# Block linear attention into an ELU feed-forward on one core: uncast loads for the first chunks, k decayed once, a plain causal mask, and a new order of all work

## The chip, the core and the metric

The kernel runs on one of the eight cores of a Trainium2 chip. A core has TensorE (PE in the profile), which multiplies matrices into PSUM; VectorE (DVE), ScalarE (ACT) and GpSimd (POOL) for elementwise work; SyncE (SP), which here only issues DMAs; and 16 DMA engines. Each engine executes its own instructions in order and waits on semaphores for the others. The metric is the device time of one execution in microseconds, lower is better.

## The reference, cut to what matters

q, k and v have 4 batches, 8 heads, 768 positions and 64 columns; `lam` is one decay per head. The output has 3072 rows (batch times position) of 512 columns.

```python
for b in range(nb):                                   # blocks of 64 positions
    intra = einsum('bhic,bhjc->bhij', qb, kb) * Dmask   # lam**(i-j) where i >= j, else 0
    intra = einsum('bhij,bhjd->bhid', intra, vb)
    inter = einsum('bhid,bhde->bhie', qb * lam_pow, kv_state)   # lam**(i+1)
    out[:, :, sl] = intra + inter
    kv_state = lam_block * kv_state + einsum('bhsd,bhse->bhde', kb * rev_pow, vb)
x = out.transpose(0, 2, 1, 3).reshape(B * S, H * D)     # 3072 x 512
h = x @ w_in                                            # 512 x 2048
g = where(h > 0, h, exp(minimum(h, 0)) - 1)
return g @ w_out                                        # 2048 x 512
```

## The kernel before

The work is cut into 24 chunks of 128 positions: chunk g is row `g // 4` of batch `g % 4`. Chunks 0 to 3 are the first row and have no incoming state. Chunks 0 to 3 are loaded and multiplied one by one, all later ones in pairs (4 and 5, 6 and 7, and so on).

For one chunk the steps are: q and k are transposed, chunks 0 to 7 on TensorE (`att_T_pe`, L274) with ScalarE copying k and VectorE multiplying q by its decay `qs`, later chunks by DMA (`att_T_dma`, L264). `att_S` (L294) computes the scores in two PSUM banks; `att_E` (L313) multiplies each by the mask, which holds the causal zeros and k's part of the decay. `att_P` (L327) multiplies by v and adds q times the state. The result is copied to `xt`. `att_kd` (L169) makes on GpSimd a second, decayed k, and `att_U` (L388) multiplies it with v for the next state; `att_M` (L368) multiplies the old state by its decay on GpSimd, and VectorE adds the two (L412).

The feed-forward takes `xt` in units. A unit `mm1(g0, j)` (L467) is eight or sixteen matmuls into one `psH` bank, for which there are two buffers; ScalarE then makes exp and relu (L484, L485), and VectorE joins them into `g` (L457). A unit `mm2(g, j)` (L490) is four matmuls of 512 columns over four tiles of g, added in one bank per chunk; four units finish a chunk, and the output is copied and stored.

w_in and w_out arrive in eight pieces each (`i0` to `i7`, `o0` to `o7`), two column tiles (row tiles for w_out) in a piece. A piece `i` serves a half of a single chunk's mm1 unit: unit j needs i(2j) and i(2j+1). A mm2 unit j needs o(2j) and o(2j+1). All these loads, and those of q, k, v, are issued by GpSimd with a cast from fp32 to fp16 on the way; the one exception is q of chunk 0, loaded uncast by SyncE and cast by VectorE.

The schedule is written by hand. `POOL_ORDER` (L47) orders GpSimd's loads (`k0`, `i0`, ...), decayed k (`d`) and state decay (`m`). `OPEN` (L53) orders the rest up to chunk 8: T, S, P, U, W, `1:g:j` and `2:g:j`; from there offsets (`AT`, L63) place each step relative to the mm1 units. VectorE's evacuations stand in a list `late` and are emitted one by one between the units. `w2` and `w6` in `OPEN` are two and six matmuls of zeros (L84), besides ten at the start. `BANKS` names the PSUM bank of each early tile.

Of the kernel before, what the change touches and what calls it, by code (L numbers as in the profile page):

```python
# [15 lines left out]
def kernel(  # L16
# [30 lines left out]
    POOL_ORDER = (  # L47
        "k0 k1 iota q1 k2 v1 i0 v0 q2 i1 v2 i2 o0 i3 d0 q3 o1 i4 k3 i5 o2 o3 v3 d1 m4 d2 d3 i7 "
        "o4 o5 i6 o7 k4 o6 q4 m5 k6 v4 q6 k10 q10 d5 d4 d6 m6 v6 k8 q8 v8 d7 m7 v10"
    )  # L50
    RAW = "q0"
    FIRST = "q0:0 c0 c1 c2"
    OPEN = (  # L53
# [7 lines left out]
    )  # L61
    LAGU = 7
    AT = {"L": -18, "W": -13, "T": -9, "S": -8, "B": -4}  # L63
    BANKS = (
        "S0=M0,M1 S1=C,D S2=D,M1 S3=D,B P0=M1 P1=B P2=B P3=D U0=M0 U1=D U2=A U3=M1 T0=M1,C "
        "T1=D,A T2=A,D T3=D T4=M0 T5=A T6=M1 T7=D M2=C M3=M0"
# [14 lines left out]
    def zero_matmuls(n):  # L81
# [4 lines left out]
    zero_matmuls(10)  # L86
# [4 lines left out]


# [3 lines left out]
    st = [  # L96
        [cpool.tile([128, NHP, 128], FP16, name=f"st{b}_{i}") for i in range(2)]
        for b in range(B)
    ]
    qg, kg, vg = {}, {}, {}  # L100

    def emit_load(w, g0):
        n = size_of[g0]
        c, b = divmod(g0, B)
        x = {"q": q, "k": k, "v": v}[w]
        src = x[b : b + n, :, c * L : (c + 1) * L].rearrange("b h p d -> p (b h) d")
        t = asb.tile([128, n, H, 64], FP16, tag=f"{w}n{n}", name=f"{w}n{g0}", bufs=4)
        {"q": qg, "k": kg, "v": vg}[w][g0] = t
        nc.gpsimd.dma_start(out=t[:].rearrange("p b h d -> p (b h) d"), in_=src)  # L109


    raw = {}
    for w in RAW.split():
        x = {"q": q, "k": k}[w[0]]
        g0 = int(w[1:])
        raw[w] = asb.tile([128, H, 64], FP32, name=f"raw_{w}", tag=f"raw_{w}")
        (nc.sync if w[0] == "q" else nc.scalar).dma_start(
            out=raw[w][:], in_=x[g0, :, 0:L].rearrange("h p d -> p h d")
        )
    nc.scalar.preload_act_table_set("natural_log_exp_and_others")  # L120

    def cast_raw(g, w, eng):
        n = f"{w}{g}"
        t = asb.tile([128, 1, H, 64], FP16, tag=f"{w}n1", name=f"{w}n{g}", bufs=4)
        (qg if w == "q" else kg)[g] = t
        if eng == 0:
            nc.vector.tensor_copy(t[:, 0], raw[n][:])
        else:
            nc.scalar.copy(t[:, 0], raw[n][:])

    def of(tiles, g):
        g0, i = group_of[g]
        return tiles[g0][:, i]
# [29 lines left out]
    def emit_iota():  # L163
        nc.gpsimd.iota(iota_c[:], pattern=[[0, 1]], base=0, channel_multiplier=1)
        nc.gpsimd.iota(iota_r[:], pattern=[[1, 128]], base=0, channel_multiplier=0)

    kds, qkT, Pt, psS, xg = {}, {}, {}, {}, {}

    def att_kd(g):  # L169
        if g // B == NCB - 1:  # L170
            return
        kd = asb.tile([128, H, 64], FP16, tag="kd", name=f"kd{g}", bufs=8)
        kds[g] = kd
        nc.gpsimd.tensor_tensor(  # L174
            out=kd[:], in0=of(kg, g),
            in1=ks[:].unsqueeze(2).broadcast_to([128, H, 64]), op=ALU.mult,
        )


    pool_list = POOL_ORDER.split()  # L180

    def emit_pool():
        w = pool_list.pop(0)
        if w == "iota":
            emit_iota()
        elif w[0] in "qkv":
            emit_load(w[0], int(w[1:]))
        else:
            {"i": emit_wi, "o": emit_wo, "d": att_kd, "m": lambda g: att_M(g)}[w[0]](int(w[1:]))

    def emit_pool_run():
        while pool_list and pool_list[0][0] != "m":
            emit_pool()

    assert "iota" in POOL_ORDER.split("d0")[0]
    while pool_list and pool_list[0][0] not in "dm":
        emit_pool()

    def zero_st1(b):
        nc.vector.memset(st[b][1][:], 0.0)  # L200


    loglam = cpool.tile([128, H], FP32, name="loglam")
    nc.scalar.activation(loglam[:], lam_b[:], AF.Ln)
    pos = cpool.tile([128, 3], FP32, name="pos")
# [4 lines left out]

    dn = cpool.tile([128, H], FP32, name="dn")
    mask = cpool.tile([128, H, 128], FP32, name="mask")
    qs = cpool.tile([128, NHP, 128], FP32, name="qs")
    ks = cpool.tile([128, H], FP32, name="ks")
    upp = cpool.tile([128, NHP], FP32, name="upp")
    nc.vector.tensor_copy(row[:], iota_r[:])
    nc.vector.tensor_copy(pos[:, 0:1], iota_c[:])
    nc.vector.tensor_scalar_mul(pos[:, 1:2], iota_c[:], -1.0)
    nc.scalar.activation(dn[:], loglam[:], AF.Exp, scale=pos[:, 1:2])
    nc.vector.tensor_scalar(  # L220
        out=ident16[:], in0=row[:], scalar1=pos[:, 0:1], scalar2=None, op0=ALU.is_equal
    )
    nc.vector.tensor_scalar(
        out=causT[:], in0=row[:], scalar1=pos[:, 0:1], scalar2=None, op0=ALU.is_ge
    )
    for hh in range(2):
        r = slice(hh * 64, (hh + 1) * 64)
        nc.vector.tensor_copy(loglam_p[r, :], loglam[r, hh::2])
    nc.vector.tensor_scalar_add(pos[:, 2:3], pos[:, 1:2], float(L))

    def emit_qs():
        for hp in range(NHP):
            nc.scalar.activation(
                qs[:, hp, :], row[:], AF.Exp, scale=loglam_p[:, hp : hp + 1]
            )

    def emit_mask():
        nc.vector.tensor_tensor(
            out=mask[:],
            in0=causT[:].unsqueeze(1).broadcast_to([128, H, 128]),  # L240
            in1=dn[:].unsqueeze(2).broadcast_to([128, H, 128]),
            op=ALU.mult,
        )

    def emit_ks():
        nc.scalar.activation(ks[:], loglam[:], AF.Exp, scale=pos[:, 2:3])
        nc.scalar.activation(upp[:], loglam_p[:], AF.Exp, scale=float(L))

# [13 lines left out]


    def att_T_dma(g):  # L264
        ts = []
        for w, tiles in (("q", qg), ("k", kg)):
            t = asb.tile([128, NHP, 128], FP16, tag=f"{w}T", name=f"{w}T{g}", bufs=6)
            nc.sync.dma_start_transpose(
                out=t[:], in_=of(tiles, g).rearrange("p h d -> p (h d)")
            )  # L270
            ts.append(t)
        qkT[g] = ts

    def att_T_pe(g):  # L274
        n = len(TAGS[f"T{g}"].split())
        pts = [
            bank(f"T{g}", i, [128, 2 // n, NHP, 128], FP16, f"psT{g}_{i}")
            for i in range(n)
        ]
        pts = [pts[0][:, 0], pts[n - 1][:, 2 // n - 1]]  # L280
        for src, pt in zip((of(qg, g), of(kg, g)), pts):
            for hp in range(NHP):
                nc.tensor.transpose(  # L283
                    pt[:, hp, :], in_=src[:, 2 * hp : 2 * hp + 2, :], identity=ident16[:]
                )
        qt, kt = [
            asb.tile([128, NHP, 128], FP16, tag=f"{w}T", name=f"{w}T{g}", bufs=6)
            for w in "qk"
        ]
        nc.vector.tensor_tensor(out=qt[:], in0=pts[0], in1=qs[:], op=ALU.mult)  # L290
        nc.scalar.copy(out=kt[:], in_=pts[1])  # L291
        qkT[g] = (qt, kt)

    def att_S(g):  # L294
        qt, kt = qkT[g]
# [11 lines left out]
    late, X_done, Y_done, E_done = [], set(), set(), set()  # L307

    def until(done, g):
        while g not in done:  # L310
            late.pop(0)()

    def att_E(g):  # L313
        pts = psS.pop(g)

        def half(hh):
            P = asb.tile([128, NHP, 128], FP16, tag="pp", name=f"pp{g}_{hh}", bufs=6)
            nc.vector.tensor_tensor(  # L318
                out=P[:], in0=pts[hh][:], in1=mask[:, hh::2, :], op=ALU.mult
            )  # L320
            Pt[(g, hh)] = P
            if hh == 1:
                E_done.add(g)

        return [lambda: half(0), lambda: half(1)]

    def att_P(g):  # L327
        cb, b = divmod(g, B)
        until(E_done, g)
        if cb > 0:  # L330
            until(Y_done, g - B)
# [331 lines left out]
```

## Time and profile before

| | us |
|---|---|
| device time, three runs | 215.18, 215.49, 215.70 (median 215.49) |
| span of the profiled execution, first to last instruction | 213.2 |
| PE busy | 202.7 (95%) |
| DVE, ACT, POOL busy | 130.1, 129.0, 96.2 |
| read from and written to HBM | 27.27 MB and 6.29 MB |

The profiled execution has no device time beside it other than these runs; its span lies 2.3 us below their median. In what follows, a row of a timeline gives the start, the length, the engine, the line, the operation, the tiles and the count of instructions that were merged; brackets at the end give idle time before it and what ended that. A row of TensorE ends some 0.17 us after its last issue, so the distance between the starts of two rows is what the first one costs.

### The profile page before, as it was taken

The page shows a single profiled execution, that of the slowest core. Times are in us where ns is not written, and L with a number is a line of the kernel's source. Part 1 is how long each engine was busy: PE and PEld are TensorE (multiplying, and loading weights), DVE is VectorE, ACT ScalarE, POOL GpSimd, SP SyncE. Part 2 cuts the span into 40 slices and gives each one's busy share as a digit, 9 for nine tenths or more (in the row PEclk, how much of TensorE's full clock was granted, in tenths as well). Part 3 has the DMA queues.
Part 4 walks back from the last instruction along what each step waited for, and adds up shares of the span by engine and source line. Part 5 has one row for each costly group of instructions (what it writes and reads, how often), then busy time and mean ns, then how long its engine had stood idle before and what let it go on. Part 6 is the DMA issues. An engine that isn't in the chain of part 4 may idle for free.

```text
span 213.2 us, 5156 instructions
## 1 busy us (share of the span) xinstructions
PE 202.7 (95%) x2066; PEld 138.1 (65%) x2066; DVE 130.1 (61%) x224; ACT 129.0 (61%) x245; POOL 96.2 (45%) x115
## 2 busy tenths in 40 slices
PE   7667999999999999999999999999999999999994
PEld 2355676767686776766766766766766666666652
DVE  3936453777846888677667667667667547533321
ACT  4545654884867756676476476476476576477640
POOL 7996991999972908667166259300000000000000
PEclk9999999999999999999999999999999999999999
DMA  8999999999996999999939919999124110110112
GB/s 90 141 175 193 192 148 173 147 165 147 153 165 145 111 197 107 144 122 116 129 106 125 167 59 103 144 180 161 52 65 83 52 49 0 54 51 16 36 49 98
DMA packets 101976, 24.59 MB, mean 115 GB/s; under 512 B 92608, under 2 KB 99008, under 8 KB 101952
## 3 DMA queue, kind: packets, MB, share of 16 engines
q0 software_dynamic: 79760, 13.50, 83.1%
q1 hardware_dynamic: 22192, 10.76, 24.6%
q8 instruction: 16, 0.26, 0.5%
q14 instruction: 8, 0.07, 0.1%
HBM read 27.27 MB, written 6.29 MB: 157 GB/s over the span
## 4 chain that ended last, share of the span: by engine, by line
PE 82%; POOL 8%; DMA 7%; issue 1%; ACT 1%; DVE 0%; POOLq 0%; ACTq 0%
PE psM L499 36%; PE psH L478 35%; DMA wi<-in_moe_w_in_dram 4%; DMA wo<-in_moe_w_out_dram 3%; PE psO L338 3%; PE psS L302 3%; PE psO L344 2%; POOL kd L174 1%; POOL wi L148 1%; POOL kn L109 1%; POOL vn L109 1%; PE psU L406 1%; PE psT L283 1%; POOL qn L109 1%; POOL wo L155 1%
## 5 line engine op out<-in xcount | busy, mean ns | idle before, releaser
L478 PE MATMUL psH<-xt,wi 128*128 128x256 f16 (+1 forms) x896 | 99.3, 258 | 2.0 <-DMA wi<-in_moe_w_in_dram 1.1
L457 DVE SCALAR_TENSOR_TENSOR g<-e,psH 128x512 f16<-128x512 f32 x96 | 65.8, 686 | 56.7 <-ACT psH L485 56.0
L484 ACT ACTIVATE e<-psH 128x512 f32<-128x512 f32 x96 | 57.3, 597 | 65.0 <-PE psH L478 62.8
L499 PE MATMUL psM<-wo,g 128*128 128x512 f16 (+1 forms) x384 | 95.6, 377 | 0.7 <-DMA wo<-in_moe_w_out_dram 0.7
L478 PEld LDWEIGHTS <-wi 128*128 128x128 f16 x896 | 76.9, 98 | 27.4 <-DMA wi<-in_moe_w_in_dram 1.8
L485 ACT ACTIVATE psH<-psH 128x512 f32<-128x512 f32 x96 | 57.0, 593 | 0.0
L499 PEld LDWEIGHTS <-g 128*128 128x128 f16 x384 | 35.9, 98 | 29.3 <-issue 1.3
L318 DVE TENSOR_TENSOR pp<-psS,mask 128x512 f16<-128x512 f32 x48 | 30.8, 684 | 4.4 <-PE psS L302 4.4
L174 POOL TENSOR_TENSOR kd<-kn,ks 128x512 f16<-128x512 f16 x20 | 20.7, 1040 | 21.3 <-DMA kn<-in_k_dram 20.4
L378 POOL TENSOR_TENSOR stt<-st,upp 64x256 f32<-64x256 f16 x32 | 19.5, 608 | 14.7 <-DVE st L418 8.9
L109 POOL DMA_DIRECT2D vn<-in_v_dram x14 | 15.5, 1108 | 1.7 <-DMA wi<-in_moe_w_in_dram 1.7
L109 POOL DMA_DIRECT2D kn<-in_k_dram x14 | 15.5, 1105 | 0.8 <-POOLq L647 0.8
L525 ACT COPY osb<-psM 128x512 f32<-128x512 f32 x23 | 13.5, 590 | 3.2 <-PE psM L499 3.2
L109 POOL DMA_DIRECT2D qn<-in_q_dram x13 | 14.8, 1138 | 0.0
L418 DVE TENSOR_TENSOR st<-stt,psU 64x256 f16<-64x256 f32 x32 | 13.3, 416 | 1.2 <-PE psU L406 0.5
L361 DVE TENSOR_TENSOR xt<-psO,qs 128x512 f16<-128x512 f32 x16 | 11.0, 688 | 3.5 <-PE psO L344 3.5
L338 PE MATMUL psO<-pp,vn 128*64 128x128 f16 x192 | 12.0, 222 | 1.2 <-DMA vn<-in_v_dram 1.0
L338 PEld LDWEIGHTS <-vn 128*64 128x64 f16 x192 | 9.7, 110 | 4.6 <-issue 2.9
L344 PE MATMUL psO<-qT,st 128*64 128x128 f16 x160 | 10.0, 219 | 0.0
L344 PEld LDWEIGHTS <-st 128*64 128x64 f16 x160 | 8.9, 110 | 0.0
L302 PE MATMUL psS<-qT,kT 64*128 64x128 f16 x192 | 7.9, 218 | 0.3 <-ACT kT L291 0.3
L359 ACT CAST xt<-psO 128x512 f16<-128x512 f32 x8 | 4.4, 588 | 6.4 <-PE psO L338 4.3
(44 smaller groups left out, 72.3 us busy)
## 6 DMA issues: line engine op xcount, KB each, us to landing
out_dram<-osb SPq DMA_DIRECT2D x23, 256.0 KB, 2.2
kn<-in_k_dram POOLq DMA_DIRECT2D x10, 256.0 KB, 7.8
qn<-in_q_dram POOLq DMA_DIRECT2D x10, 256.0 KB, 6.8
vn<-in_v_dram POOLq DMA_DIRECT2D x10, 256.0 KB, 7.6
wi<-in_moe_w_in_dram POOLq DMA_DIRECT2D x8, 256.0 KB, 6.9
wo<-in_moe_w_out_dram POOLq DMA_DIRECT2D x8, 256.0 KB, 7.7
kn<-in_k_dram POOLq DMA_DIRECT2D x4, 128.0 KB, 4.2
vn<-in_v_dram POOLq DMA_DIRECT2D x4, 128.0 KB, 5.5
```

The source lines that it names most:

```text
L109: nc.gpsimd.dma_start(out=t[:].rearrange("p b h d -> p (b h) d"), in_=src)
L174: nc.gpsimd.tensor_tensor(out=kd[:], in0=of(kg, g), in1=ks[:].unsqueeze(2).broadcast_to([128, H, 64]), op=ALU.mult,)
L302: nc.tensor.matmul(psS[g][hh][:, hp, :], lhsT=kt[r, hp, :], rhs=qt[r, hp, :], start=True, stop=True,)
L318: nc.vector.tensor_tensor(out=P[:], in0=pts[hh][:], in1=mask[:, hh::2, :], op=ALU.mult)
L338: nc.tensor.matmul(po[r, hp, :], lhsT=vt[:, 2 * hp + hh, :], rhs=Pt[(g, hh)][:, hp, :], start=True, stop=(cb == 0), skip_group_check=True,)
L344: nc.tensor.matmul(po[r, hp, :], lhsT=st[b][cb % 2][:, hp, r], rhs=qt[:, hp, :], start=False, stop=True, skip_group_check=True,)
L378: nc.gpsimd.tensor_tensor(out=tmp[r], in0=old[r, :, r], in1=upp[r].unsqueeze(2).broadcast_to([64, NHP, 64]), op=ALU.mult,)
L457: nc.vector.scalar_tensor_tensor(out=g[:].rearrange("p f c t -> p (f c t)"), in0=e[:], scalar=-1.0, in1=r[:], op0=ALU.add, op1=ALU.min,)
L478: nc.tensor.matmul(pH[:, f * n * 128 : (f + 1) * n * 128], lhsT=wi16[i][:, kk, w * 128 : (w + 1) * 128], rhs=xg[g0][:, kk, :], start=(kk = ...
L484: nc.scalar.activation(e[:], pH[:], AF.Exp)
L485: nc.scalar.activation(pH[:], pH[:], AF.Relu)
L499: nc.tensor.matmul(psM[g][:, cols], lhsT=gts[(g, j * FB + f)], rhs=wo16[i][:, w, cols], start=first and f == 0, stop=end and f == FB - 1, ...
```

## The change

Four things change. q of chunks 0 to 3 (SyncE's queue) and k of chunks 0 and 1 (ScalarE's queue) are loaded uncast and multiplied by their decay on VectorE or GpSimd (`scaled`). The decayed k is also what is transposed for the scores, so k's decay is made once, and its base is the chunk's end; the mask is then causal alone, the same for all heads. The state is added first (`att_Y`, VectorE) and multiplied by the decay after that (`att_M`, GpSimd). And one list, `ORDER`, gives the place of every step of every engine, with no offsets and no `late`; it has no zero matmuls but the ten at the start. `BANKS` names all banks.

The tokens of `ORDER`: `L:k2` a cast load, `i:3` and `o:4` weight pieces, `a:q1:v` uncast q or k times decay (`v` VectorE, `p` GpSimd, `a` ScalarE, here and below), `d:5:p` decayed k from a cast k, `t:k4` and `D:k8` a transpose on TensorE or by DMA, `e:k4:a` the transpose's copy out of PSUM, `s`, `p`, `u` the TensorE steps S, P and U, `E:4:1` one half of the mask, `x` the copy to `xt`, `y` and `m` the two steps of the state, `z` zeros into a state tile, `1:g:j` and `2:g:j` the units, `g:g:j` the joining into g. The other words are constants.

```diff
-    RAW = "q0"
+    ZEROS = 10
+    RAW = "q0S k0A q1S k1A q2S q3S"
+    ORDER = (
+        "z:2:1:a i:3 L:k2 iota L:v1 log row col caus ks logp ident a:k0:v t:k0 qn a:q0:p z:0:1:a t:q0 e:k0:a "
+        "a:q1:v L:v0 e:q0:a a:k1:p i:2 L:k3 s:0 E:0:1 i:1 t:q1 e:q1:a i:0 qs:2 L:v2 i:4 i:5 t:k1 e:k1:a E:0:0 "
+        "L:k4 qs:3 a:q2:v s:1 E:1:1 z:1:1:a qs:0 E:1:0 d:2:v L:q4 t:q2 u:1 a:q3:v L:v3 z:1:0:v i:6 e:q2:a p:1 "
+        "t:k2 u:0 upp x:1:a p:0 i:7 L:v4 t:q3 y:1 L:q6 o:4 d:5:p e:k2:a s:2 y:0 o:5 L:k6 o:0 o:2 E:2:0 E:2:1 "
+        "x:0:a o:3 d:3:v 1:0:1 1:1:1 g:0:1 o:1 t:k3 e:q3:v e:k3:a 1:0:0 g:1:1 p:2 d:7:p u:2 1:1:0 x:2:v o:6 "
+        "y:2 s:3 g:0:0 1:0:2 E:3:0 g:1:0 E:3:1 o:7 1:2:0 d:4:v t:k4 t:k5 e:k4:a g:0:2 L:k8 qs:1 L:q8 g:2:0 "
+        "z:3:1:v e:k5:a 1:2:1 t:q4 D:q8 t:q5 e:q4:v e:q5:v 1:1:2 u:3 p:3 x:3:a s:5 g:2:1 E:5:0 s:4 1:0:3 "
+        "g:1:2 L:q10 E:4:1 1:2:2 E:4:0 u:4 g:0:3 p:4 u:5 1:3:3 E:5:1 t:q7 g:2:2 x:4:v L:v6 t:q6 y:3 z:0:0:v "
+        "g:3:3 d:9:p e:q6:v 1:3:2 L:v8 g:3:2 p:5 y:5 x:5:a y:4 L:q12 L:k12 d:8:p 2:2:2 1:3:0 d:6:v L:k10 "
+        "1:1:3 2:0:2 t:k7 g:3:0 g:1:3 t:k6 2:1:2 1:2:3 1:3:1 L:v12 2:2:1 2:0:0 g:2:3 g:3:1 1:4:2 D:q9 2:0:1 "
...
+        "2:4:2 g:6:4 2:6:0 2:5:1 y:7 m:7 2:6:2 g:6:7 2:6:1 D:k11 m:9 2:4:3 1:8:0 s:10 s:11 E:10:0 E:10:1 "
+        "g:8:0 E:11:0 2:6:3 E:11:1 1:8:1 g:8:1 2:7:0 1:8:2 g:8:2 2:7:1 1:8:3 d:12:p D:q12 D:k12 g:8:3 1:8:4 "
...
+    )
...
+    for w in RAW.split():
+        g0 = int(w[1:-1])
+        raw[w[:-1]] = asb.tile([128, H, 64], FP32, name=f"raw_{w[:-1]}", tag=f"raw_{w[:-1]}")
+        {"S": nc.sync, "A": nc.scalar}[w[-1]].dma_start(
+            out=raw[w[:-1]][:], in_=xin[w[0]][g0, :, 0:L].rearrange("h p d -> p h d")
+        )
...
+    def scaled(w, g, eng):
+
+        t = asb.tile([128, H, 64], FP16, tag="kd" if w == "k" else "qd", name=f"{w}d{g}", bufs=8 if w == "k" else 4)
+        {"v": nc.vector, "p": nc.gpsimd}[eng].tensor_tensor(
+            out=t[:], in0=raw[f"{w}{g}"][:],
+            in1=(ks if w == "k" else qn)[:].unsqueeze(2).broadcast_to([128, H, 64]), op=ALU.mult,
+        )
...
+    def att_T_pe(w, g):
+        pt = bank(f"T{w}{g}", 0, [128, NHP, 128], FP16, f"psT{w}{g}")
+        src = of("q", g) if w == "q" else kds[g][:]
...
-                out=P[:], in0=pts[hh][:], in1=mask[:, hh::2, :], op=ALU.mult
...
+    def att_E(g, hh):
+        P = asb.tile([128, NHP, 128], FP16, tag="pp", name=f"pp{g}_{hh}", bufs=6)
+        nc.vector.tensor_tensor(
+            out=P[:], in0=psS[g][hh][:],
+            in1=causT[:].unsqueeze(1).broadcast_to([128, NHP, 128]), op=ALU.mult,
+        )
...
+            nc.gpsimd.tensor_tensor(
+                out=new[r, :, r], in0=stt.pop((g, hh))[r],
+                in1=upp[r].unsqueeze(2).broadcast_to([64, NHP, 64]), op=ALU.mult,
+            )
+
+    def att_Y(g, hh):
...
+        if cb == 0:
+            nc.vector.tensor_tensor(
+                out=stp[b][1][r, :, r], in0=src,
+                in1=upp[r].unsqueeze(2).broadcast_to([64, NHP, 64]), op=ALU.mult,
+            )
+        else:
+            tmp = asb.tile([128, NHP, 64], FP32, tag="stt", name=f"stt{g}_{hh}", bufs=8)
+            nc.vector.tensor_tensor(
+                out=tmp[r], in0=stp[b][cb % 2][r, :, r], in1=src, op=ALU.add
+            )
...
+    for t in ORDER.split():
+        run(t)
+    mm2_rest()
+    emit_stores()
```

More of the change, by code (lines that the diff above doesn't have):

```diff
@@ L161 @@
     iota_r = cpool.tile([128, 128], I32, name="iota_r")
[L163 to L200, printed above, removed]
     loglam = cpool.tile([128, H], FP32, name="loglam")
-    nc.scalar.activation(loglam[:], lam_b[:], AF.Ln)
-    pos = cpool.tile([128, 3], FP32, name="pos")
+    col = cpool.tile([128, 2], FP32, name="col")
     row = cpool.tile([128, 128], FP32, name="row")
@@ L219 @@
[L219 to L242, printed above, removed]
[L243 to L247 removed]
+    def emit_iota():
+        nc.gpsimd.iota(iota_c[:], pattern=[[0, 1]], base=-L, channel_multiplier=1)
+        nc.gpsimd.iota(iota_r[:], pattern=[[1, 128]], base=-L, channel_multiplier=0)
@@ L305, in att_S @@
                 )
[L307 to L318, printed above, removed]
-                out=P[:], in0=pts[hh][:], in1=mask[:, hh::2, :], op=ALU.mult
[L320 to L325, printed above, removed]
+    def att_E(g, hh):
[4 more added lines that the diff above has]
+        )
+        Pt[(g, hh)] = P
     def att_P(g):
         cb, b = divmod(g, B)
-        until(E_done, g)
-        if cb > 0:
-            until(Y_done, g - B)
-        vt = of(vg, g)
-        qt, _ = qkT[g]
+        vt = of("v", g)
+        qt = qkT[("q", g)]
         po = bank(f"P{g}", 0, [128, NHP, 128], FP32, f"psO{g}")
@@ L397, in att_U @@
+    def att_U(g):
+        if g < B:
+            pu = bank(f"U{g}", 0, [128, NHP, 64], FP32, f"psU{g}")
+        elif g % 2 == 0:
+            psUU[g] = bank(f"U{g}", 0, [128, 2, NHP, 64], FP32, f"psU{g}")
+            pu = psUU[g][:, 0]
+        else:
+            pu = psUU[g - 1][:, 1]
+        vt = of("v", g)
+        for hp in range(NHP):
+            for hh in range(2):
+                r = slice(hh * 64, (hh + 1) * 64)
                 nc.tensor.matmul(
-                    full[:, hp, :].rearrange("p (h e) -> p h e", h=2),
@@ L585 @@
-    for t in FIRST.split():
-        run(t)
-    emit_pool_run()
-    prog = OPEN.split()
-    done = set(prog) | {o for t in prog if t[0] == "B" for o in t.split(":")}
-    m1 = [(g, j) for g, n in GSIZE.items() for j in range(NJ * n)]
-    place = {u: i for i, u in enumerate(m1)}
-    need = {
-        (g, j): place[(GFIRST[g], ((j + 1) * FB - 1) // (FB // GSIZE[GFIRST[g]]))]
-        for g in range(NG) for j in range(NJ)
-    }
-    m2 = [(g, j) for g in range(NG) for j in range(NJ) if f"2:{g}:{j}" not in done]
@@ L612 @@
-    m1 = [x for x in m1 if "1:%d:%d" % x not in done]
-    first = place[m1[0]]
-    for p in sorted(extra):
-        if p < first:
-            prog += extra.pop(p)
-    for x, (g, j) in enumerate(m1):
-        u = first + x
-        prog.append(f"1:{g}:{j}")
-        prog += extra.pop(u, [])
-        n = 2
-        while m2 and need[m2[0]] <= u - 2 and n and len(m2) - (len(m1) - 1 - x) > LAGU:
-            prog.append("2:%d:%d" % m2.pop(0))
-            n -= 1
-    for g, j in m2:
-        prog.append(f"2:{g}:{j}")
```

354 lines of the change are left out of this document (130 added, 224 removed), and 41 rows, old and new, of tables (BANKS, OPEN, ORDER).

## The prediction

> **What bounds the kernel now.** I read the page first, then the chain of waits, then the timeline engine by engine, and last the time from issue to landing of each load. Page, 40 slices of 5.33 us:
>
> ```profile
> PE   7667999999999999999999999999999999999994
> PEclk9999999999999999999999999999999999999999
> DMA  8999999999996999999939919999124110110112
> ```
>
> TensorE is full from the fifth slice on, at full clock. Before that it is short of work, while the DMA engines are full for the first 64 us. The chain of waits says for what:
>
> ```profile
> 11.63 8.79 DMA wi<-in_moe_w_in_dram
> ...
> 27.49 6.73 DMA wo<-in_moe_w_out_dram
> 34.26 1.46 PE psM L499 x6
> ```
>
> The TensorE timeline: the first w_in product starts at 13.37 us, the last wait over 0.25 us on a load ends at 34.26, and from then on rows follow each other, with one gap of 0.22 us at 87.
>
> ```profile
> 13.37 0.61 PE L478 MATMUL psH<-xt,wi 128*128 128x128 f16 x8
> ...
> 34.26 1.46 PE L499 MATMUL psM<-wo,g 128*128 128x512 f16 x6 [0.35 <-DMA wo<-in_moe_w_out_dram]
> ...
> 43.23 0.39 PE L283 MATMUL psT<-ident,kn 128*128 128x128 f16 x4
> 43.45 1.03 PE L499 MATMUL psM<-wo,g 128*128 128x512 f16 x4
> ```
>
> So the span is the opening plus a remainder that runs at TensorE's pace. From chunk 8 on the new order is regular, with the same matmuls, and I cost that at nothing. It is hidden by TensorE being full: VectorE (130.1 us) and ScalarE (129.0) are busy 61% of the span; with that cover gone each extra 0.69 us VectorE operation would show. The question is how much TensorE work is done by some mark past the opening. I take 43.45 us, after the transposes of chunks 4 and 5.
>
> **Prices.** A mm1 unit of 16 matmuls (chunks 0 to 3) issues in 0.89 us (36.72 to 37.62 in the timeline), a mm2 unit in 0.867, a chunk's eight transposes in 0.45, a chunk's S or P in 0.23. The psH tile goes round in 2.0 us from the last issue of its unit to g:
>
> ```profile
> 19.11 0.60 ACT L484 ACTIVATE e<-psH 128x512 f32<-128x512 f32 x1 [1.14 <-PE psH L478]
> 19.60 0.59 ACT L485 ACTIVATE psH<-psH 128x512 f32<-128x512 f32 x1
> 20.23 0.69 DVE L457 SCALAR_TENSOR_TENSOR g<-e,psH 128x512 f16<-128x512 f32 x1 [1.17 <-ACT psH L485]
> ```
>
> (first unit issued 18.02 to 18.91, g done 20.92). psH has two buffers, so a mm1 unit waits for the g of the unit two before it. Loads: successive landings (v0 12.05, q2 12.9; o5 34.2, i6 35.6, o7 36.9; o6 40.1, q4 41.8) give 0.85 us of DMA service for a 128-token load of q, k or v, 1.35 for a weight pair, 1.75 for a two-chunk load.
>
> **Uncast loads.** Of the six, q0 was uncast before; five issues of 0.9 us leave GpSimd, 4.6 us in all. Do they cost less service? They read the same bytes. The only row is raw_q: issued 1.19, landed after 3.3 us, against 4.0 for the cast k0; bounds for one load are 0 (a path of its own) and 0.85. I take 0.85, since the engines are already full in the second slice and raw_q shared them with k0. The Trainium skill, page "DMA: Bandwidth & Descriptors", section "Issuing engines are not separate DMA queues", says that issuing from several engines saves only sequencer time; the full DMA row agrees, and with separate paths 5 us of service would go and the sum would fall well below what follows.
>
> Cast in software the values came ready; now they are multiplied by decay from fp32: k0, q1, q2, q3 on VectorE, q0 and k1 on GpSimd. No such row; bounds 0.60 (half of the 128x1024 mask, 1.20) and 1.04 (kd on GpSimd); I take 0.65 on VectorE, next to pp (0.684, 0.62 back to back), 1.04 on GpSimd.
>
> **k with decay once, mask.** S now needs kd, so each PE transpose of k stands behind a kd: GpSimd's d5 waits in its queue for k4's landing with o5 and k6 behind it, d7 for k6's with o6, o7 behind it. Four more kd for the last chunks, 1.04 us each on GpSimd with 96.2 us busy: hidden. The 1.20 us mask goes; pp reads a 128x128 mask broadcast, same size of work, 0 (bounds −0.1 to +0.1). U of chunks 0 to 3 becomes eight half-wide matmuls, 0.11 instead of 0.23. State: VectorE adds, GpSimd scales (two of 0.608), needed one chunk row later: hidden. The eight zero matmuls between go; they sat in idle time: 0.
>
> **Walk of the new opening.** Landings by service order, allowing before's pace: v0 13.2, i2 14.5, k3 15.4, i0 18.1, v2 18.9, i5 21.6, k4 23.4, q4 25.2, i7 28.8 to 29.3, q6 32.3 to 32.9, o5 35.0 to 35.5, k6 36.8, o1 42.1 to 42.8. The two-chunk loads k4, q4, v4, q6, k6 (8.75 us of service) now stand ahead of wo pairs.
> TensorE is in order: t:q3 and P0 stand before the first mm1. v0 13.2, P0 13.35, q3 scaled 13.7, S2 14.25, x:0 on ScalarE (0.588) 14.8: first mm1 at 14.85, 1.5 us later than now. On VectorE d2, a:q3, y1, y0, E2 (two), d3 (waits for k3) then run until 17.5, so g:0:1 ends 18.2 and 1:0:0 starts 18.25. The next units follow g: 1:0:2 at 21.75 (behind y2), 1:2:1 at 24.9 (behind d4, k4), 1:0:3 at 28.85 to 29.3 (i7), 1:3:3 at 31.7 to 32.25, 1:3:2 at 33.15 to 33.65 (behind q6's transposes), P5 to 34.6 or 35.0, and the first mm2, 2:2:2, at 35.05 to 35.5 (o5). From there TensorE is full: 1:3:0, 1:1:3, 2:0:2, t:k7, t:k6, 2:1:2, 1:2:3, 1:3:1, 2:2:1, 2:0:0, ending at 43.5 to 44.1; I take 43.8.
>
> **Balance.** By 43.45 the present kernel has issued 15 mm1 units, 10 mm2 units, transposes of six chunks, S and P of four, U of three. By 43.8 the new one has 16 mm1, 5 mm2, eight chunks transposed, S, P and U of six. It owes five mm2 units (4.33) and has ahead: 0.89, transposes 0.90, S of 4 and 5 0.68 (45.30 to 45.98), U3 and the burst of chunks 4 and 5 1.59 (48.58 to 50.17), together 4.06. It is 0.27 behind, 0.35 later: +0.6 us. Behind the mark I find no new wait: q8's landing (48.2) and the transposes on SyncE precede S9 at 57. Span 213.2 + 0.6 = 213.8; the median 215.49 is 2.3 above the span of the profiled execution, so 216.1. Of the 16 us in which TensorE has no useful work up to the mark (43.45 less 27.3 at these prices), the change shifts the place, not the amount: loads are served at the same rate, and the early mm1 work is bought with late mm2 work.
>
> **Rivals.**
> Loads ahead of my table, faster. Up to o7 the present loads need 12 x 0.85 + 15 x 1.35 = 30.5 us of service; from a start at 2.9 and some 1.2 to the semaphore that is 34.6, but o7 landed at 36.9. The 2.3 us were lost where GpSimd stood still:
>
> ```profile
> 20.70 0.89 POOL L109 DMA_DIRECT2D vn<-in_v_dram  x1 [1.66 <-DMA wi<-in_moe_w_in_dram]
> ```
>
> and again before 25.98 (kd behind k3). (v3 had to wait for i3, eight loads before it.) The new order issues 19 loads before the first kd on GpSimd that waits for a cast load. If 1.5 us of it is won, o5 lands by 34.0, 1:0:3 follows g at 28.05, and 2:2:2 comes at 34.0 to 34.3: 1.3 us earlier, span 212.5, time 214.8; with all of it and VectorE at 0.62 throughout, 214. It decides if o5 lands before 34.3. Against it: GpSimd still stops for k4 and k6, and for the load eight places back. Chance 0.30.
> VectorE becomes the bound, slower still. Up to the mark it would carry some 26 operations of 0.65, 15 g of 0.69, six y pairs of 0.87: 33 us out of 39, where the present one carries 24 (its busy time in windows of 5 us). If the new forms cost 0.75 or more, g comes later at each of the round trips: 26 x 0.1 is up to 2.6, half of it on the path, 217.4. Chance 0.16.
> TensorE cools, slower still. Zeros took 0.40 us each in the first 4 us and 0.245 in the row "9.57 1.47 x6"; without the fill a mm1 unit could take 1.78 instead of 0.89. Four steps ahead of the first mm1 (0.2 each) and two units, partly behind g: 0.7 to 2.0 us, 217.5. For it: TensorE would work a quarter of the time from 5.2 to 14 us. Against: my walk has no idle stretch over 1.3 us, and one of 1.31 at 7.95 left the clock at 1.00. The Trainium skill, "TensorE: Matmul & The Clock Gate", Part 1, has the half clock return after an idle window of some 3.4 us; by that rule it would not here. Chance 0.12.
> That the loads stay serial whatever the queue is in the forecast already.
>
> **How the numbers follow.** Forecast 0.42, range of its own 215.3 to 217.0; likeliest 216.1. Range 213.9 to 218.2: down into the faster case, up through both slower ones. 0.2% (0.43 us) is about what a measurement can tell from no change: below 215.06 lies most of the first rival and a little of the forecast, 0.31; between, 0.16; above 215.92, 0.53.
>
> **What would show it.** First mm1 near 14.9 us; 2:2:2 near 35.3 with o5's landing just ahead; TensorE full from there; 2:0:0 ending near 43.8. If 2:2:2 starts before 34.3 the first rival holds; if the idle time before psH rows names g, VectorE; if the granted clock drops between 5 and 20 us, the third. I am wrong altogether if TensorE waits again between 44 and 65 us.

## The result and the profile after

The changed kernel takes 222.92 us (median of four runs, 221.62 to 224.94) against 215.34 (215.03 to 215.7) for the kernel before beside it: a ratio of 1.0364, interval 1.0305 to 1.0423. It is slower, as forecast, but by 7.6 us where 0.6 was forecast, and outside the range. The profiled execution is the longest of the four, 224.94 us with a span of 223.2, so its trace shows about 2 us more than the median run lost. Of e2, e5 and e10 below, one execution in four was slow (223.17, 225.45 and 222.66 us), and their medians and ratios are those of the other three.

The same three rows of the page, now in slices of 5.58 us:

```profile
PE   7269899999939999999999999999999999999994
PEclk9755999999997999999999999999999999999999
DMA  4999999999999001631999959939969921100112
```

Three things are new: a poorer opening at half clock, a hole in PE in the twelfth slice with the clock down behind it, and idle DMA engines just after that. From there on the row is as full as before. The chain of waits (start, duration, what) names what ended last at both places:

```profile
1.67 9.32 DMA raw_q<-in_q_dram
...
56.45 9.24 DMA kT<-kd
```

So the end now hangs, before the first product, on an uncast load of q, and later on a transpose of decayed k that takes 9.24 us. The TensorE timeline gives the price: the first w_in product at 18.89 us (forecast 14.85), the first w_out product, 2:2:2, at 38.85 (35.05 to 35.5), and in front of S of chunks 9 and 8 two waits of 3.8 us together where none was expected:

```profile
18.89 3.49 PE L433 MATMUL psH<-xt,wi 128*128 128x128 f16 x32
...
38.85 1.04 PE L453 MATMUL psM<-wo,g 128*128 128x512 f16 x4
...
62.67 0.40 PE L310 MATMUL psS<-qT,kT 64*128 64x128 f16 x8 [1.12 <-DMA kT<-kd]
...
65.74 0.40 PE L310 MATMUL psS<-qT,kT 64*128 64x128 f16 x8 [2.67 <-DMA kT<-kd]
```

The opening on SyncE, GpSimd and VectorE: the four issues of raw_q last 7.15 us (the last two 3.10 and 2.93), and q1's multiplication starts at 11.08, VectorE having stood 4.73 us for its load:

```profile
1.21 7.15 SPq L137 DMA_DIRECT2D raw_q<-in_q_dram  x4
7.05 1.04 POOL L245 TENSOR_TENSOR qd<-raw_q,qn 128x512 f16<-128x512 f32 x1 [2.71 <-DMA raw_q<-in_q_dram]
11.08 0.69 DVE L245 TENSOR_TENSOR qd<-raw_q,qn 128x512 f16<-128x512 f32 x1 [4.73 <-DMA raw_q<-in_q_dram]
```

Busy time by stretch of the kernel after (stretch, its length, PE, PEld, DVE, ACT, POOL, then granted clock, DMA share, GB/s); in the kernel before, TensorE was busy 3.37 us of the second stretch and all of the last, at full clock:

```profile
5.00:10.00 5.00, 1.82 (x18) 0.89 (x16) 1.01 (x3) 1.66 (x4) 2.93 (x4) 0.85 1.41 202
10.00:15.00 5.00, 2.15 (x22) 1.50 (x24) 3.05 (x5) 2.26 (x6) 5.00 (x8) 0.50 1.70 184
...
60.00:70.00 10.00, 6.21 (x90) 3.94 (x89) 3.22 (x6) 3.19 (x6) 1.29 (x3) 0.83 1.82 168
```

### The profile page after: what moved, and what is told of

The parts are those of the page before. It is cut to its first block, busy times and chain, and to the rows that moved or that the text cites. A ratio compares the mean times of both kernels' runs of the same rounds, so it can differ in the third digit from the quotient of the medians.

```text
span 223.2 us, 5160 instructions
## 1 busy us (share of the span) xinstructions
PE 207.0 (93%) x2074; PEld 142.0 (64%) x2074; DVE 132.6 (59%) x230; ACT 129.8 (58%) x245; POOL 91.1 (41%) x109
## 4 chain that ended last, share of the span: by engine, by line
PE 76%; DMA 8%; DVE 8%; ACT 4%; issue 2%; POOL 0%; SPq 0%; DVEq 0%; ACTq 0%
PE psM L453 34%; PE psH L433 33%; DMA raw_q<-in_q_dram 4%; DMA kT<-kd 4%; DVE g L418 3%; PE psO L331 3%; PE psS L310 3%; PE psO L337 2%; DVE pp L317 2%; ACT e L439 1%; ACT psH L440 1%; PE psU L401 1%; DVE stt L384 1%; ACT kT L299 1%; DVE stp L378 1%
## 5 line engine op out<-in xcount | busy, mean ns | idle before, releaser
L433 PE MATMUL psH<-xt,wi 128*128 128x256 f16 (+1 forms) x896 | 101.7, 262 | 1.2 <-DVE g L418 0.8
L368 POOL TENSOR_TENSOR stp<-stt,upp 64x256 f16<-64x256 f32 x32 | 19.5, 610 | 50.3 <-DVE stt L384 48.6
L317 DVE TENSOR_TENSOR pp<-psS,causT 128x512 f16<-128x512 f32 x48 | 31.1, 684 | 11.5 <-PE psS L310 11.4
L257 POOL TENSOR_TENSOR kd<-kn,ks 128x512 f16<-128x512 f16 x17 | 17.5, 1044 | 25.6 <-DMA kn<-in_k_dram 13.8
L148 POOL DMA_DIRECT2D kn<-in_k_dram x12 | 13.4, 1117 | 0.7 <-DMA vn<-in_v_dram 0.5
L384 DVE TENSOR_TENSOR stt<-stp,psU 64x256 f32<-64x256 f16 x32 | 13.3, 416 | 0.6
L148 POOL DMA_DIRECT2D qn<-in_q_dram x10 | 11.8, 1181 | 0.9 <-DMA wi<-in_moe_w_in_dram 0.7
L310 PEld LDWEIGHTS <-kT 64*128 64x128 f16 x192 | 5.8, 98 | 8.7 <-DMA kT<-kd 4.5
L337 PE MATMUL psO<-qT,stp 128*64 128x128 f16 x160 | 10.8, 225 | 0.0
L337 PEld LDWEIGHTS <-stp 128*64 128x64 f16 x160 | 9.2, 113 | 0.0
```

Of the source, the lines that this page charges most:

```text
L257: {"v": nc.vector, "p": nc.gpsimd}[eng].tensor_tensor(out=kd[:], in0=of("k", g), in1=ks[:].unsqueeze(2).broadcast_to([128, H, 64]), op=ALU ...
L310: nc.tensor.matmul(psS[g][hh][:, hp, :], lhsT=kt[r, hp, :], rhs=qt[r, hp, :], start=True, stop=True,)
L317: nc.vector.tensor_tensor(out=P[:], in0=psS[g][hh][:], in1=causT[:].unsqueeze(1).broadcast_to([128, NHP, 128]), op=ALU.mult,)
L337: nc.tensor.matmul(po[r, hp, :], lhsT=stp[b][cb % 2][:, hp, r], rhs=qt[:, hp, :], start=False, stop=True, skip_group_check=True,)
L368: nc.gpsimd.tensor_tensor(out=new[r, :, r], in0=stt.pop((g, hh))[r], in1=upp[r].unsqueeze(2).broadcast_to([64, NHP, 64]), op=ALU.mult,)
L433: nc.tensor.matmul(pH[:, f * n * 128 : (f + 1) * n * 128], lhsT=wi16[i][:, kk, w * 128 : (w + 1) * 128], rhs=xg[g0][:, kk, :], start=(kk = ...
```

## The experiments

The profile after leaves two questions. For the opening: theory A, the uncast loads come late and everything queues behind them; against it B, the cold clock costs the time. For the hole at 60 to 71 us there are two candidates. C: the transposes of k share the DMA engines with five pair loads that the new order issues at the same time. D: they are issued too late on SyncE, behind others. In later runs A2 is A in its sharper form, V says that VectorE's queue sets the opening, I that GpSimd's issue time does. All ratios are to the kernel before, run beside each.

**e1: TensorE kept busy.** The changed kernel with 25 zero matmuls put between the steps of the opening:

```diff
-ident a:k0:v t:k0 qn ...  t:q0 e:k0:a ...  s:0 E:0:1 ...  t:k1 e:k1:a ...  u:1 a:q3:v
+ident a:k0:v t:k0 w:5 qn ...  t:q0 w:3 e:k0:a ...  s:0 w:9 E:0:1 ...  t:k1 w:5 e:k1:a ...  u:1 w:3 a:q3:v
```

> The changed kernel with zero matmuls put back into TensorE's waits: 5 after the transpose of k0, 3 after that of q0, 9 after S0, 5 after the transpose of k1, 3 after U1. In the changed kernel the granted clock is half from about 9 to 21 us, and the first w_in product starts at 18.89 us. Theory A (the loads are late, the cold clock costs little): the clock stays at 1.00, the first w_in product comes near 17.4 us, but the first w_out product (38.85 us now) is held by w_out piece o5, which lands near 37.9 us, so it moves by at most 0.9 us; time 222.0 to 222.9. Theory B (the cold clock is the opening's loss): the first w_out product comes 3 us earlier or more, time 218.5 to 220. The wait at 60 to 71 us stays in both.

Measured: 224.12 us, 1.0418 (1.0364 to 1.0471). The clock stayed at 1.00 through the opening, yet 2:2:2 came at 38.29 instead of 38.85:

```profile
10.00:15.00 5.00, 4.46 (x40) 2.10 (x40) 3.08 (x5) 2.26 (x7) 5.00 (x7) 1.00 1.70 183
```

At that place some half a microsecond belongs to the clock. The time gained nothing and lies 1.2 us above theory A's range, which stays unexplained. B, which wanted 3 us or more at 2:2:2, falls: the cold clock is not what makes the opening late.

**e2: the five pair loads later.**

```diff
-... y:4 L:q12 L:k12 d:8:p 2:2:2 1:3:0 d:6:v L:k10 ... 1:3:1 L:v12 ... g:4:0 L:v10 ... g:4:6 m:5
+... y:4 d:8:p 2:2:2 1:3:0 d:6:v ... 1:3:1 ... g:4:0 ... g:4:6 m:5 L:q12 L:k12 L:k10 L:v12 L:v10
```

> The changed kernel with five pair loads (q12, k12, k10, v12, v10) moved on GpSimd from around d8 to behind m5, so that d8 comes directly behind d9. Theory C (S9 and S8 at 62.7 and 65.7 us wait for k transposes that share the DMA engines with these loads and take 7.6 and 9.2 us to land, against 2.4 to 3.9 before): the transposes land within 5 us, the wait before S9 falls from 3.8 us in all to under 1, the clock does not dip at 66, and the time falls by 4 to 5 us to about 218.3. Theory D (the transposes are late because SyncE issues them behind a store that waits for its data until 54.6 us): the issue stays at 55.05 and so does most of the wait, time 221.5 to 223.

**e3: the transposes of k issued earlier.**

```diff
-... 1:4:2 D:q9 2:0:1 ... E:7:1 D:k9 E:7:0 2:1:1 D:k8 2:3:1
+... 1:4:2 D:q9 D:k9 D:k8 2:0:1 ... E:7:1 E:7:0 2:1:1 2:3:1
```

> The changed kernel with the DMA transposes of k9 and k8 moved ahead of the store on SyncE (directly behind those of q8 and q9); the loads on GpSimd stay. Theory C (contention with the loads): k9's transpose is issued 1.7 us earlier, k8's waits for d8 (55.3) anyway and lands near 64, the wait before S9 and S8 falls by at most 1.5 us, time 221.5 to 222.5. Theory D (the order on SyncE): both are issued before 56 and land by 60, the wait goes, time near 218.5.

Measured: e2 219.82 us, 1.0221 (1.0169 to 1.0272); e3 220.70, 1.0253 (1.0194 to 1.0311). Each takes 2 to 3 us off and neither the 4 to 5 that its own theory forecast, so each cause is real and, as e7 below shows, they overlap. In e3 one of the two waits before S9 and S8 is left, and the clock stays at 1.00:

```profile
62.99 0.40 PE L310 MATMUL psS<-qT,kT 64*128 64x128 f16 x8 [0.99 <-DMA kT<-kd]
```

**e4: the kernel before without its eight fill matmuls.**

```diff
-"... T0 w2 T1 S0 S1 w6 P0 P1 ..."
+"... T0 T1 S0 S1 P0 P1 ..."
```

> The kernel before without its eight zero matmuls between the steps of the opening (w2 and w6). If the clock falls without them as in the changed kernel, the granted clock shows a half somewhere between 6 and 20 us. Theory A (a cold clock costs little since the opening waits for loads): time 215.3 to 216.5, with the first w_out product at most 0.5 us later. Theory B (the cold clock is the loss): 217.5 or more. If TensorE's short steps alone keep the clock up, nothing changes: 215.1 to 215.6.

Measured: 214.92 us, 0.9997 (0.997 to 1.0025). The granted clock fell to 0.50 at 10 to 15 us and 0.82 at 15 to 20, and the median did not move. The first w_out product came 0.56 us later (21.48 against 20.92), about what theory A allowed. Dropping the zeros costs no time that can be measured, even where it does cool TensorE.

**e5: five loads cast again.**

```diff
-RAW = "q0S k0A q1S k1A q2S q3S"
+RAW = "q0S"
-z:2:1:a i:3 L:k2 iota L:v1 log ...  L:v0 e:q0:a a:k1:p ...
+z:2:1:a L:k0 L:k1 iota L:q1 i:3 L:k2 L:v1 L:q2 log ...  L:v0 L:q3 e:q0:a d:1:p ...
```

> k0, k1, q1, q2 and q3 go back to loads that cast in software, issued by GpSimd in about the order of the kernel before; only q0 stays uncast, and its tile is multiplied from fp32 as before. Everything behind the opening is as in the changed kernel. Theory A (the five uncast loads on the hardware queues make every later landing about 2.5 us late): the first w_in product comes near 15 to 16 us instead of 18.9, the first w_out product (unit 2:2:2) near 36 instead of 38.85, and the time falls by 2 to 3.5 us, to 219.5 to 221; the wait for kT between 60 and 71 us stays, but may grow by what the opening gives, since the transposes wait for loads whose issue is tied to GpSimd's own queue. Rival (the loads are late because of the order of issues on GpSimd, the w_in pairs ahead of v0 and so on, not because five loads are uncast): first w_in product stays at 18 or later and the time moves by less than 1 us.

Measured: 222.54 us, 1.0344 (1.0298 to 1.0391), first w_in product at 18.82, 2:2:2 at 38.66. This is the rival's result (its reason is not shown by it), and a miss for theory A as it then stood: with the uncast loads gone, the opening is as late as with them. Yet the early loads are not: v0 landed at 13.33 us here and at 15.76 in the changed kernel (a landing is a load's issue plus its time from issue to landing in the DMA view).

**e6: uncast, but issued by GpSimd.**

```diff
-RAW = "q0S k0A q1S k1A q2S q3S"
+RAW = "q0S k0P q1P k1P q2P q3P"
-{"S": nc.sync, "A": nc.scalar}[w[-1]].dma_start(
+{"S": nc.sync, "P": nc.gpsimd}[w[-1]].dma_start(
```

> The same six loads stay uncast, in fp32, but k0, q1, k1, q2 and q3 are issued by GpSimd's queue, ahead of all its other loads, instead of by SyncE and ScalarE; the order of everything else is that of the changed kernel. It tells whether the missing time is in the uncast form (fp32 tiles, 512 KB written per load of 128 tokens instead of 256) or in the hardware queues. If the queues: q1 to q3 land within 4 us of each other's service as other loads of GpSimd do, first w_in product near 16, 2:2:2 near 36.5, time 220 to 221.5. If the form: landings as in the changed kernel or later by the 4.6 us of issues that GpSimd has to make first, first w_in product at 19 or later, time 222.5 to 226.

Measured: 224.55 us, 1.045 (1.0405 to 1.0494), first w_in product at 20.16, 2:2:2 at 39.58. Time and product are those of the second branch, but the landings are not: the last of the six came at 10.63 us instead of 15.24, and v0 at 14.06 instead of 15.76. GpSimd's queue moved the five loads in 320 packets of 4 KB, and they landed 1.2 us apart. The edit also put GpSimd's seven first issues in front of its iota, from which the decay and the identity are made: k0 had landed at 5.87, and its multiplication started at 10.05 (5.66 in the changed kernel). So e6 does not separate the form from the queues. (The sizes in the expectation are too large by two: a tile of 128 tokens is 256 KB in fp32 and 128 in fp16.)

**e7: e2 and e3 together.** Both diffs above.

> The edits of e2 (five pair loads issued behind m:5) and e3 (the transposes of k of chunks 8 and 9 directly behind that of q on SyncE) together; the opening is that of the changed kernel. Theory C plus D (the hole at 60 to 71 us has two parts, transposes that are issued behind waiting ones and transposes that share the DMA engines with five pair loads): no wait for kT over 0.5 us is left in 60 to 71, the clock stays at 1.00 there, and the time is 218 to 219, 4 to 5 us below the changed kernel. If one of them alone does it: no better than e2 (220.0).

Measured: 219.74 us, 1.0196 (1.0169 to 1.0224). Groups by tile kT, how long TensorE's S stood for it (us, times) and the time from issue to landing; first the changed kernel, then e7:

```profile
  DMA kT<-kd: 8.2, 4
...
DMA to landing us min/median/max: 2.4/2.4/9.2
```

```profile
  DMA kT<-kd: 0.2, 1
...
DMA to landing us min/median/max: 2.4/2.4/4.7
```

The wait is gone, and with it 3.2 us, less than the 4 to 5 of the forecast; in time e7 can't be told from e2. The opening is untouched (2:2:2 at 39.02).

**e8: e5 and e7 together.**

> e5 and e7 together: cast loads in the opening and the transposes freed. If the two faults (late opening, wait for kT) are the whole loss, what is left is the forecast's sum without its price for the uncast loads: TensorE full from about 36 us, time 214.5 to 216.5, the same as the kernel before within 1 us. If a third cause is left in the new order, 217 or more.

Measured: 219.26 us, 1.0184 (1.016 to 1.0207): e7's time again. A third cause was left, as the second branch had it.

**e9: the same bytes in fewer pieces.** On e7:

```diff
-in_=xin[w[0]][g0, :, 0:L].rearrange("h p d -> p h d")
+in_=xin[w[0]][g0].rearrange("h s d -> (h s) d")[0 : 8 * L].rearrange("(p x) d -> p x d", x=8)
```

> e7 (transposes freed), and the six uncast loads read 128 pieces of 2 KB that lie one after the other in memory instead of 1024 of 256 B: as many bytes, other values, so what is computed for the first chunks is not the reference's. Theory A2 (the landings of the uncast loads, and of all that queues behind them, set the opening): SyncE's blocked issues go, q1 to q3 land before 9 us instead of 11.05 to 15.2, the first w_in product comes at 16 to 17 instead of 19.1, unit 2:2:2 at 36 to 37 instead of 39.0, and the time falls 2 to 3 us below e7's 219.7. Theory V (from about 14 us on the work queued on VectorE in its order sets the opening, and would with any landing seen so far): less than 1 us, and VectorE's busy share from 25 to 40 us stays over 90%.

Measured: 216.30 us, 1.0057 (1.0032 to 1.0083). First w_in product at 15.88, 2:2:2 at 35.16, inside the forecast's 35.05 to 35.5, and 2:2:1 with 2:0:0, forecast to end near 43.8, are the eight that start at 42.30 and end their issue at 44.02:

```profile
15.88 2.12 PE L434 MATMUL psH<-xt,wi 128*128 128x128 f16 x32
...
35.16 1.04 PE L454 MATMUL psM<-wo,g 128*128 128x512 f16 x4
...
42.30 1.89 PE L454 MATMUL psM<-wo,g 128*128 128x512 f16 x8
```

All of this is a little better than A2 forecast (16 to 17, 36 to 37, and 2 to 3 us). v0 shows where it comes from; its issue and the time from issue to landing, in the changed kernel (issued at 8.04) and in e9 (7.51):

```profile
vn<-in_v_dram POOLq DMA_DIRECT2D x1, 128.0 KB, 7.7
```

```profile
vn<-in_v_dram POOLq DMA_DIRECT2D x1, 128.0 KB, 5.0
```

**e10: less on VectorE.** On e7, `y:0`, `y:1`, `y:2` and `y:3` taken out of the order.

> e7 without the four pairs of VectorE operations (0.85 us a pair, 3.4 us in all, two of them ahead of the first w_in product) that write the state of the first four chunks; the state stays zero, so later chunks of that sequence are computed without it. Loads are untouched. Theory V: unit 2:2:2 comes 1.5 to 2.5 us earlier than in e7 (39.0), the time falls by as much, to 217.5 to 218. Theory A2 (loads): 2:2:2 stays within 0.5 us, time 219.3 to 219.8.

Measured: 218.68 us, 1.0158 (1.0108 to 1.0208); 2:2:2 at 38.01. That is 1.0 us earlier, between the two forecasts. VectorE was busy 14.21 of the 15 us from 25 to 40 in e7, and still 13.81 here: a full engine, but not the one that everything waited for.

**e11: e9 and e10 together.**

> e9 and e10 together, with both parts left out as told there. If loads and VectorE each hold the opening at nearly the same time, either alone gives little and both together give 3 us or more: 216.5 or less. If one of them is the bound alone, no better than the better of the two.

Measured: 215.93 us, 1.0045 (1.0021 to 1.0069), within e9's interval; 2:2:2 came at 36.11 here, 0.95 us later than in e9 although less was done. The traces of the changed kernel, e3 and e7, which share one opening, lie within 0.2 us there (38.85 to 39.02), so that difference is not known to be scatter, and its cause stays open. With the loads in time, the work on VectorE is worth nothing that can be told.

**e12: one product earlier.** On e7:

```diff
-upp x:1:a p:0 ... E:2:0 E:2:1 x:0:a o:3 d:3:v 1:0:1 1:1:1 g:0:1 ... 1:0:0 g:1:1 p:2
+upp x:1:a 1:1:1 p:0 ... g:1:1 E:2:0 E:2:1 x:0:a o:3 d:3:v 1:0:1 g:0:1 ... 1:0:0 p:2
```

> e7 with one w_in unit (1:1:1, chunk 1, whose input is the first to be ready) put directly behind x:1 on TensorE instead of behind P0, the transposes of q3, S2 and the first unit of chunk 0, with its g ahead of E2 on VectorE. Everything is still computed. If the order on TensorE is what makes the products start late, they start at 17.2 to 17.5 instead of 19.1 and the time falls by up to 1.5 us; if VectorE or the loads hold the stretch behind, 2:2:2 stays within 0.4 us of 39.0 and so does the time within 0.5 of 219.7.

Measured: 221.51 us, 1.0285 (1.0226 to 1.0344), slower than e7. The first product came at 17.53, but 2:2:2 at 40.78. The unit took 1.89 us at half clock, in front of P0 and S2, and the half clock lasted longer: 0.50 from 20 to 25 us, where e7 has 0.91. How much each cost was not separated.

**e13: cast loads, and GpSimd relieved.** e8 with two multiplications moved:

```diff
-a:q0:p ... d:1:p
+a:q0:v ... d:1:v
```

> e8 (cast loads in the opening, transposes freed) with the two multiplications that GpSimd makes between its early loads (q0 and k1 by decay, 1.1 us each) given to VectorE, which is idle there from 6.4 to 10.9 us. Theory I (with cast loads the opening is held by GpSimd's time: five more issues of 0.9 us and these two): v0 and all later loads are issued 1.1 to 2.2 us earlier, the first w_in product comes at 16.8 to 17.8 instead of 18.8, 2:2:2 at 36.7 to 37.6 instead of 38.65, the time is 217.2 to 218.2 against 219.3 for e8. Rival (the DMA engines serve cast loads no faster, so the issue time is hidden): landings and time within 0.5 us of e8.

Measured: 217.63 us, 1.0108 (1.007 to 1.0147), first w_in product at 16.41, 2:2:2 at 36.15, earlier than forecast for them. GpSimd's timeline, e8 first (the multiplications L245 and L257 between its issues), then the same loads in e13:

```profile
7.80 1.11 POOL L245 TENSOR_TENSOR qd<-raw_q,qn 128x512 f16<-128x512 f32 x1
8.79 0.95 POOL L148 DMA_DIRECT2D vn<-in_v_dram  x1
9.73 0.89 POOL L148 DMA_DIRECT2D qn<-in_q_dram  x1
10.62 1.07 POOL L257 TENSOR_TENSOR kd<-kn,ks 128x512 f16<-128x512 f16 x1
11.61 0.82 POOL L167 DMA_DIRECT2D wi<-in_moe_w_in_dram  x1
```

```profile
7.77 0.94 POOL L148 DMA_DIRECT2D vn<-in_v_dram  x1
8.63 0.95 POOL L148 DMA_DIRECT2D qn<-in_q_dram  x1
9.49 0.84 POOL L167 DMA_DIRECT2D wi<-in_moe_w_in_dram  x1
```

That resolves e5 in the main: there GpSimd's time took the place of the DMA engines' time. Theory I had v0 and all later loads earlier. v0 did not move (13.47 in e8, 13.42 here) and o5 landed 0.8 us earlier (37.25, 36.48), which is not the whole. The two multiplications themselves, which GpSimd reaches only behind its issues, stand in front of TensorE's first steps: S of chunk 0 starts at 10.26 in e8 and at 7.78 in e13.

The same move was not tried with the uncast loads. The trace after gives it little: TensorE stood 2.00 us until 11.83 for q1's multiplication, and GpSimd had ended that of k1 at 10.06.

**e14: k0 uncast as well.** e13 with `RAW = "q0S k0A"`, and `a:k0:v` for `d:0:v`.

> As e13, with k0 uncast on ScalarE's queue as well, so that two of the six are uncast and four cast. By theory I one issue of 0.9 us less on GpSimd is worth up to 0.9 us; by theory A2 an uncast load of 1024 pieces costs the engines 1.2 to 1.4 us against 0.85 to 1.0 for a cast one. Together: 216.5 to 218, within 0.7 us of e13, and the best order of the loads that still computes everything. Not faster than the kernel before.

Measured: 217.27 us, 1.0106 (1.0067 to 1.0145): the same as e13, and 2:2:2 at 36.41. The loads land earlier than in e13 (v0 at 12.70 against 13.42, o5 at 35.54 against 36.48), so it is not a dearer load that cancels the issue saved; what holds the opening there was not found.

**e15: pieces of 512 B.** On e7:

```diff
-out=raw[w[:-1]][:], in_=xin[w[0]][g0, :, 0:L].rearrange("h p d -> p h d")
+out=raw[w[:-1]][:].rearrange("p (x t) d -> p x t d", t=2),
+in_=xin[w[0]][g0].rearrange("h s d -> (h s) d")[0 : 8 * L].rearrange("(x p t) d -> p x t d", p=128, t=2)
```

> e7 with the six uncast loads cut into 512 pieces of 512 B each, between the 1024 of 256 B of e7 and the 128 of 2 KB of e9; as many bytes, other rows in each piece, so the values of the first chunks are not the reference's. If the number of pieces is the price, the packets of the six loads take 5.5 to 7 us of the 16 engines (8.8 in e7, 4.85 in e9), the first w_out product comes between 35.9 and 37.8 us (39.0 and 35.2), and the time is 217 to 218.5 (219.7 and 216.3). If instead it was that e9 reads one run of memory per load, e15, which jumps between pieces as far as e7 does, stays near e7: over 219.

Measured: 217.93 us, 1.0143 (1.0097 to 1.019), 2:2:2 at 36.80. The DMA queues in the first 16 us (packets, MB, share of that time of 16 engines), q1 SyncE's and q10 ScalarE's: the changed kernel, e15, e9. With them goes a small load of lam.

```profile
q1 hardware_dynamic: 4304, 1.05, 39.7%
q10 hardware_dynamic: 2080, 0.52, 15.2%
```

```profile
q1 hardware_dynamic: 2256, 1.05, 30.4%
q10 hardware_dynamic: 1056, 0.52, 12.7%
```

```profile
q1 hardware_dynamic: 720, 1.05, 20.0%
q10 hardware_dynamic: 288, 0.52, 10.3%
```

The bytes are equal, the packets are not. In time of the 16 engines: 54.9% of 16 us is 8.8 us, 43.1% is 6.9, 30.3% is 4.85. Steps of 1.9 and 2.05 us; v0's landing moved from e7's 16.00 by 1.9 and 1.6 (14.10, 12.54), 2:2:2 from 39.02 by 2.2 and 1.6. For one layout the number of pieces, with their size, is the price: e15 and e9 read the same run of 256 KB for a load. e7 reads eight runs of 32 KB, 192 KB apart, so its step to e15, which the expectation took to jump as far, holds a change of layout too. SyncE's four issues took 7.15 us in the changed kernel, 2.82 in e15 and 2.14 in e9: the first step may hold some of that, the second hardly, so it is not the blocked issue alone. How the first step divides between pieces, layout and blocked issue was not tried.

None of these kernels beats the kernel before. The best that compute everything, e13 and e14, are 1.1% behind it.

## Why the prediction was right or wrong

**The direction** was right, but by luck for the most part: what made the kernel slower is two things that the sum put at nothing or too low, not the 0.27 and 0.35 us that its balance found. With both out of the way the sum holds: e9, where the loads have few pieces (and bring other values) and the transposes are in time, takes 216.3 us where 216.1 was forecast. In ratios, which allow for other chips, the forecast was 1.003 and e9 is 1.0057 (1.0032 to 1.0083); some 0.6 us of extra loss stays unexplained. Of the 3.6% in all, the wait for the transposes is 1.7 (1.0364 to 1.0196, e7), the pieces with their layout 1.4 (1.0196 to 1.0057, e9), the rest 0.6. That e9 met 2:2:2 so closely is in part luck: v0 landed 0.7 us earlier than forecast there, the first product came 1.0 later, and the way from it to 2:2:2 was 1.2 shorter (19.28).

**"I take 0.85" for an uncast load: the step that failed in the opening.** The bounds, 0 and 0.85, left out that it could cost more than a cast load, and 0.85 was taken from successive landings of other loads, on another path. The trace of before had a nearer row, SyncE's queue in its first 16 us, nearly all of it raw_q:

```profile
q1 hardware_dynamic: 1184, 0.27, 7.6%
```

That is 1.2 us of 16 engines for one load; in the changed kernel six took 8.8, or 1.46 each. Such a share orders loads of one form, but it can't be set against 0.85, because packets overlap. GpSimd's queue alone comes to more than the engines' whole time in the same stretch of the kernel before, where a cast load is 1024 packets too (of 128 B, 32 ns each: 2.0 us a load):

```profile
q0 software_dynamic: 9963, 1.90, 142.8%
```

Landings can be set against it. Cast loads landed 0.85 us apart in e5 as well (v1, q2, v0, q3 from 11.61 to 14.17). The uncast ones landed 1.2 apart in e6. In the changed kernel k0 landed at 5.56 and q3 at 15.24; with i3, k2 and v1, which landed between, at the prediction's prices (3.05 us), that leaves an estimated 1.33 us for each of five. So the step is a term of the sum that was mis-sized, 0.85 for 1.33: 0.48 us on five loads is 2.4 us, and v0 landed at 15.76 instead of 13.2. From there to o5 the forecast's 21.8 to 22.3 us held (22.16). In e9 the uncast loads landed 0.87 apart, and v0 at 12.54.

The first product was 4.0 us late, of which v0's landing is 2.6. The rest is a second, smaller miss in the walk: from v0 to the first product it had 1.65 us, and the traces have 3.1 (3.3 in e9). From the first product to 2:2:2 its 20.45 us held (19.96).

The Trainium skill, "DMA: Bandwidth & Descriptors", section "Why small descriptors are slow (HBM only)", states a fixed overhead for each piece, 27% at 256 B on this chip. The direction agrees; here 256 B took 1.8 times as much packet time as 2 KB (8.8 against 4.85 us).

**"Five issues of 0.9 us leave GpSimd"** was right, and this is why e5 gained nothing: cast, the loads held up GpSimd and the multiplications behind them; uncast, they took more of the DMA engines' time. The sum priced the gift and not its counterpart.

**"Behind the mark I find no new wait" failed**, worth 3.2 us in the medians. Steps that were moved were followed by their engine, not with what they issue. In the trace after, GpSimd starts decayed k of chunk 9 at 49.75, its transpose waits on SyncE until 55.05, behind the two of q and a store, and then takes 7.6 and 9.2 us to land for the pair, against a median of 2.7 for k (the longest 7.9) in the kernel before, among pair loads whose issues start from 51.95 to 57.6. The prediction's last sentence, that TensorE waiting again between 44 and 65 us would make it wrong altogether, caught it.

**Loads ahead of the table (0.30)** went the other way, later by some 2.5 us. **VectorE the bound (0.16)**: its new forms cost 0.69, inside the bounds, and e10 and e11 put the share of the 3.4 us that they take off it at 1.0 us at most. **TensorE cools (0.12)** happened but cost some 0.56 us at 2:2:2 (e1, one trace); e4 shows the clock fall at no cost. The use made of the Trainium skill's rule was wrong, though: from 5.0 to 8.5 us TensorE was busy 1.17 us, no idle time was longer than 1.34, and the granted clock was 0.50 from 8.5 on. An idle window of 3.4 us ("TensorE: Matmul & The Clock Gate", Part 1 of the Trainium skill) is not needed as uninterrupted idle time; the measurement decides.

The single multiplications by decay, the mask and the regular part cost about what the sum said: 0.69 us on VectorE for 0.65, 1.04 on GpSimd, and 0.684. U of chunk 2, at full clock, took 0.22 us (e9) instead of 0.11. From 71 us on TensorE is full at the old pace.

## What to carry to other kernels

Price a load by its pieces as well as its bytes and by how far apart such loads land, not by the share of a queue, which overlaps with others; and never let the upper bound of an unknown be the price of the thing it replaces. Work taken from an issuing engine can come back on the DMA engines, and removing one of two such limits shows nothing until the other is eased (e5 against e13). When an order is changed, follow each DMA that a moved step issues, through its queue to its landing, past the loads that the same order sends at that moment.

## What the runs showed of the hardware that was not expected

- SyncE's third and fourth uncast load, of 1024 pieces each, held its queue for 3.10 and 2.93 us; with 512 pieces all four issues took 2.82 us.
- Loads of 128 tokens, 256 KB read, landed 0.85 us apart when GpSimd's queue cast them (e5) and 1.2 apart when it did not (e6, packets of 4 KB); uncast on the hardware queues 0.87 apart in pieces of 2 KB (e9), and an estimated 1.33 each in pieces of 256 B.
- The transposes of decayed k land in 2.4 us in the median of the run, but took 7.6 and 9.2 us among pair loads; the kernel before has one of 7.9 that nothing waited for.
- The granted clock fell to half after 3.5 us in which TensorE was busy a third of the time, again at 66.5 us after 0.83 us of work in 3.5, and in e1 keeping it at full in the opening moved the first w_out product by 0.56 us, while the time did not fall.
